# Chunked attention and a gated feed-forward network on one core: the down projection of the last 3584 tokens done with seven products instead of eight

## The chip, the cores and the metric

The kernel runs on one core of one Trainium2 chip. The metric is the device time of one execution in microseconds (us). TensorE (PE) multiplies matrices, VectorE (DVE), ScalarE (ACT) and GpSimd (POOL) work on elements, SyncE (SP) and ScalarE issue the transfers (DMA). The times of the kernel before are the median of three runs; everything that is said of single instructions comes from one profiled execution.

## The reference

The reference is, cut to what is computed:

```python
scores = scale * np.matmul(q_c, k_c.transpose(0, 1, 2, 4, 3))   # q, k, v: 8 x 8 heads x 576 x 64,
scores = scores - np.max(scores, axis=-1, keepdims=True)        # in chunks of 64 tokens
attn = np.exp(scores)
attn = attn / (np.sum(attn, axis=-1, keepdims=True) + 1e-09)
x = merge_heads(np.matmul(attn, v_c))                           # 4608 tokens x 512
h = x @ w_in                                                    # 512 x 2048
sp = np.where(h > 20.0, h, np.log1p(np.exp(np.minimum(h, 20.0))))
g = h * np.tanh(sp)                                             # Mish
return (g @ w_out).astype(np.float32)                           # 2048 x 512
```

The weights arrive as 64-bit words and are made into floats on the chip.

## The kernel before

**Precision.** Every large product is made of three matmuls on numbers that are split into a high part (a rounded copy, made by ScalarE) and a low part (what the copy left, a subtraction by VectorE): high by high, high by low, low by high. So each operand of a matmul costs one copy and one subtraction (`g_hi`, `g_lo`; `x_hi`, `x_lo`; `s_hi`, `s_lo`; `t_hi`, `t_lo`).

**Plain stage, the first 1024 tokens.** They go in two blocks of 512 tokens. A slot (`slot`, L811) takes one of the 16 strips of 128 hidden units: TensorE multiplies the tokens by the strip of w_in into `h` (`up`, L308, 12 matmuls of 512 columns), ScalarE applies Mish, the result is split, and one slot later TensorE adds its share of the output into `o_o` (`down`, L346, 12 matmuls). In the first block's slots the weights are also brought in and split. In the second block's slots, the sums of w_in that the next stage needs are made (`t_sum` and `t_diff` on GpSimd, `t_hi`, `t_lo`), and all split weights are written back to DRAM (`keep_weights`, `dwi`, `dwo`).

**Seven-product stage, the last 3584 tokens.** They go in four blocks of 896 tokens, each cut into two halves of 448. For a pair of 128-unit strips of w_in (a set; 8 sets a block, 32 in all) the product of 2 x 2 blocks is made from seven products instead of eight (`s_up`, L686; its matmuls stand at L699, 6 of 448 columns for each product). The operands of the seven products are sums of the blocks of x (`x_sum`, made once for each block of tokens) and of w_in. Their results are added up partly in PSUM, partly by VectorE (`s_copy` on ScalarE and `s_c`, L775, on VectorE); out come four pieces of h, called 11, 12, 21 and 22, each of 128 units by 448 tokens. Each gets Mish and is split (`s_hi`, L784 and L785; `s_lo`, L788). The down projection is plain here: for each of the 7 tiles of 128 tokens, 6 matmuls of 512 columns (`s_down`, L716; matmuls at L721) give the set's share of the output, which VectorE adds to a running sum (`s_out`, L748; in a block's first set ScalarE copies it instead, L746).

**What sets the order.** The order is written out by hand. The table `ORDER` has 14 steps for a set: seven products of the up projection with seven groups of the down projection of earlier sets in between, so that TensorE has a group of down work between any two products. `plan_set` (L919) hangs each element-wise operation on a step. `plan_x` (L937) hangs the conversion of the next block of x on the last set of a block: there GpSimd makes the sums and four of the seven low parts. `plan_pair` (L950) hangs the attention of ten later pairs of token tiles on steps of the running sets. Each engine works through its own instructions strictly in that order. The weights of the up projection come back from DRAM in groups of four products (`ring_load`), those of the down projection once for each set (`wo_load`), all by SyncE's queue.

## Time and profile before

| | |
|---|---|
| median of the three runs | 844.61 us (843.84 to 846.90) |
| the profiled execution's own time | 842.41 us |
| its span, first to last instruction | 840.6 us |
| TensorE busy | 829.7 us, 99% |
| VectorE busy | 507.0 us, 60% |
| ScalarE busy | 419.9 us, 50% |
| GpSimd busy | 111.0 us, 13% |
| transfers | 170.82 MB, 203 GB/s on average |
| granted TensorE clock | 1.00 all through |

In a row of the profile's groups stand the line, the engine, the operation, output and inputs by the program's names, the shapes, how often it occurs, its busy time and the mean of one in ns, and behind the last bar the idle time of the engine just ahead of it. "PEld" is the loading of TensorE's weights, which runs beside its matmuls. In the chain of waits and in a timeline a row gives start and duration in us. A window's row gives the busy time of each engine in that stretch.

### The profile page before, as it was taken

Reading aid. Unit: us, or ns where it says so; the run is one execution under the profiler, and the core shown is the slowest. Engines: PE = TensorE matmul, PEld = TensorE weight load, DVE = VectorE, ACT = ScalarE, POOL = GpSimd, SP = SyncE. Lnnn points to the kernel's source line nnn. Section 1 sums busy time; section 2 is a strip of 40 time slices with the busy share of each in tenths; the row PEclk is TensorE's granted clock in tenths of the full one; section 3 lists DMA queues with packets and bytes.
Section 4 is the critical chain, followed back from the end, with each engine's and each line's share of the span. In section 5 each row is a group of like instructions: output and inputs, shape, how many; then the busy total and the mean of one; then the engine's idle time right before and its main releaser. Section 6 shows DMA issues by size and latency. Waiting matters only on the chain.

```text
span 840.6 us, 14583 instructions
## 1 busy us (share of the span) xinstructions
PE 829.7 (99%) x5974; PEld 706.9 (84%) x5974; DVE 507.0 (60%) x784; ACT 419.9 (50%) x702; POOL 111.0 (13%) x83
## 2 busy tenths in 40 slices
PE   8999999999999999999999999999999999999997
PEld 7778878888888888888888888888888888888886
DVE  6898875666845656574555556544656563445444
ACT  6988855245573535554635545363535544433321
POOL 2100072652000000340000024100000440000000
PEclk9999999999999999999999999999999999999999
DMA  8767778988774644547545434764544456444413
GB/s 304 249 176 241 229 243 292 348 275 302 236 256 168 228 157 182 201 159 257 225 176 201 177 121 147 276 245 166 228 156 180 151 161 227 150 154 163 179 57 87
DMA packets 51298, 170.82 MB, mean 203 GB/s; under 512 B 5152, under 2 KB 11296, under 8 KB 39968
## 3 DMA queue, kind: packets, MB, share of 16 engines
q1 hardware_dynamic: 50384, 168.45, 57.5%
q10 hardware_dynamic: 848, 1.44, 0.4%
q8 instruction: 47, 0.77, 0.4%
q14 instruction: 19, 0.16, 0.0%
HBM read 137.36 MB, written 32.51 MB: 202 GB/s over the span
## 4 chain that ended last, share of the span: by engine, by line
PE 88%; DVE 4%; ACT 4%; DMA 2%; issue 2%; POOL 0%; ACTq 0%; POOLq 0%
PE d L721 36%; PE al L699 19%; PE g L699 9%; PE o_o L346 7%; PE h L308 6%; PE b L699 5%; PE av L182 2%; PE s L182 2%; PE pt L604 1%; DVE w L137 1%; DVE woc L126 1%; PE pt L251 1%; DMA wos<-in_w_out 1%; DMA wis<-in_w_in 1%; ACT woc L104 1%
## 5 line engine op out<-in xcount | busy, mean ns | idle before, releaser
L721 PE MATMUL d<-wo,g 128*128 128x512 f32 x1320 | 338.8, 392 | 0.0
L721 PEld LDWEIGHTS d<-wo,g 128*128 128x128 f32 x1320 | 247.9, 188 | 44.5
L748 DVE TENSOR_TENSOR sum<-d,sum 128x512 f32<-128x512 f32 x192 | 132.6, 691 | 185.7 <-PE d L721 184.9
L699 PE MATMUL al<-xo,ring 128*128 128x448 f32 x768 | 178.0, 367 | 0.0
L699 PEld LDWEIGHTS al<-xo,ring 128*128 128x128 f32 x768 | 142.4, 188 | 18.4 <-DVE c L775 0.7
L308 PE MATMUL h<-x,w 128*128 128x512 f32 (+1 forms) x396 | 93.9, 386 | 1.3 <-ACT x L282 0.8
L699 PE MATMUL g<-xo,ring 128*128 128x448 f32 x372 | 85.8, 366 | 0.0
L308 PEld LDWEIGHTS h<-x,w 128*128 128x128 f32 x396 | 71.8, 188 | 15.9 <-ACT x L282 0.9
L346 PE MATMUL o_o<-w,gh 128*128 128x512 f32 x256 | 79.0, 390 | 0.0
L699 PEld LDWEIGHTS g<-xo,ring 128*128 128x128 f32 x372 | 69.5, 188 | 8.4
L648 POOL TENSOR_TENSOR xs<-x 128x896 f32<-128x896 f32 x3 | 6.4, 2119 | 389.5 <-ACT x L545 389.5
L346 PEld LDWEIGHTS o_o<-w,gh 128*128 128x128 f32 x256 | 48.1, 188 | 9.7
L784 ACT ACTIVATE b<-b 128x448 f32<-128x448 f32 x31 | 16.4, 528 | 73.9 <-DVE b L775 73.9
L346 PE MATMUL o_o<-w,gl 128*128 128x512 f32 x128 | 50.8, 397 | 1.4 <-DVE gl L333 1.4
L784 ACT ACTIVATE g<-g 128x448 f32<-128x448 f32 x31 | 16.4, 528 | 69.8 <-DVE g L775 69.8
L699 PE MATMUL b<-xo,ring 128*128 128x448 f32 x186 | 43.4, 369 | 0.0
L784 ACT ACTIVATE c<-c 128x448 f32<-128x448 f32 x34 | 19.7, 578 | 37.1 <-DVE c L775 37.1
L699 PEld LDWEIGHTS b<-xo,ring 128*128 128x128 f32 x186 | 34.3, 188 | 3.6
L763 ACT COPY p<-al 128x448 f32<-128x448 f32 x32 | 17.1, 533 | 37.5 <-PE al L699 37.3
L494 POOL TENSOR_TENSOR c<-w 128x512 f32<-128x512 f32 x16 | 23.9, 1508 | 84.3 <-DVE w L137 84.3
L333 DVE TENSOR_TENSOR gl<-z,gh 128x512 fp32r<-128x512 f32 x32 | 27.7, 864 | 11.3 <-ACT gh L326 10.7
L775 DVE TENSOR_TENSOR b<-b,p 128x448 f32<-128x448 f32 x31 | 19.5, 629 | 22.7 <-PE b L699 22.2
(110 smaller groups left out, 985.3 us busy)
## 6 DMA issues: line engine op xcount, KB each, us to landing
ring<-dwi SPq DMA_DIRECT2D x56, 1024.0 KB, 4.9
wo<-dwo SPq DMA_DIRECT2D x32, 1024.0 KB, 4.8
wis<-in_w_in SPq DMA_DIRECT2D x16, 512.0 KB, 4.7
wos<-in_w_out SPq DMA_DIRECT2D x16, 512.0 KB, 3.7
q<-in_q SPq DMA_DIRECT2D x16, 512.0 KB, 5.9
k<-in_k SPq DMA_DIRECT2D x16, 512.0 KB, 6.7
v<-in_v SPq DMA_DIRECT2D x16, 512.0 KB, 5.8
dwo<-w SPq DMA_DIRECT2D x16, 512.0 KB, 6.8
```

Of the source, the lines that this page charges most:

```text
L104: nc.scalar.activation(out=c.bitcast(F32), in_=a[:, :, 1].bitcast(F32), func=AF.Copy, scale=2.0**-112)
L182: nc.tensor.matmul(o[h * CHUNK : (h + 1) * CHUNK, c, t - ts.start, g], lhsT=l[rows, t, 2 * g + h], rhs=r[rows, t, 2 * g + h], start=True, ...
L308: nc.tensor.matmul(h[:, cols], lhsT=wi(f, w_, kt), rhs=x[:, kt, cols], start=(n == 0), stop=(n == 3 * NK - 1),)
L333: nc.vector.tensor_tensor(out=d["gl"], in0=d["z"], in1=d["gh"].bitcast(F32), op=ALU.subtract)
L346: nc.tensor.matmul(acc[t], lhsT=g[:, sl], rhs=w_part(f, w_), start=(f == 0 and n == 0), stop=(f == NF - 1 and n == 2),)
L494: nc.gpsimd.tensor_tensor(out=d[e], in0=raw(w_part(f, 0)), in1=raw(w_part(f, 1)), op=ALU.add)
L699: nc.tensor.matmul(o[:, :HALF], lhsT=w_[:, wn, kt * P : (kt + 1) * P], rhs=x[:, xn, kt], start=(n == 0 and k < 3), stop=(n == 5), skip_gro ...
L721: nc.tensor.matmul(o, lhsT=g_tile(z, e)[:, gn, i * P : (i + 1) * P], rhs=wos[z % 2][:, e, wn], start=(n == 0), stop=(n == 5),)
L748: nc.vector.tensor_tensor(out=a, in0=o, in1=a, op=ALU.add)
L763: nc.scalar.copy(out=o, in_=(places["g"] if n == "p5" else places["a", z])[:, :HALF])
L775: nc.vector.tensor_tensor(out=ct[z, n], in0=o[:, :HALF], in1=ct.pop((z, other)), op=ALU.add)
L784: nc.scalar.activation(out=ct[z, n], in_=ct[z, n], func=AF.Mish)
```

## The change

**The down projection.** It now uses seven products of 2 x 2 blocks too. Its operands are sums of the four pieces of a set: T1 = 12 - 22, T3 = a copy of 11 - 12, T2 = that copy - T1, T4 = 21 - T2 (`s_t`), so a set now yields seven split pieces (11, 21, 22, T1 to T4) where there were four. Three of the low parts, T2 and T3 are made by GpSimd (`on_pool`), the rest by VectorE. The matching sums of w_out are made in the plain stage with those of w_in (`t_sum` now on VectorE and for both matrices, `t_diff` on GpSimd). The weights are now the stationary operand, so the output comes out turned: two sets together take 14 groups, each of 6 matmuls of 448 columns (`s_down(n)`), in the order `DOWN`; each is added to a running total by `s_out`, and in a block's last pair of sets VectorE also transposes it in squares of 32 before it is stored (`s_store`). The output columns of w_out are regrouped to suit this (`w_cols`).

**The order.** The up products of a set go in the order 0 1 3 2 5 4 6. The down groups of a pair of sets start 3 steps into the second set behind it, so the first two sets have no down group but those left over from the plain stage, and 15 groups stand alone at the end. The next block of x is converted over two sets, with all low parts and three of the four sums on VectorE.

**Plain stage.** In the second block Mish is applied in place in PSUM and `g_hi` is always ScalarE's; tiles have become views of fixed rooms.

On TensorE, in the middle of the seven-product stage, `al`, `b` and `g` are the up projection's banks and `d` the down projection's. Before:

```order
L699 MATMUL al_4483<-xo_2403,ring_2268 128x448 x6
L721 MATMUL d_2631<-wo_2481,g_2493 128x512 x3
L721 MATMUL d_2631<-wo_2481,g_2550 128x512 x3
L699 MATMUL b<-xo_2406,ring_2268 128x448 x6
L721 MATMUL d_2632<-wo_2646,g_2658 128x512 x3
L721 MATMUL d_2632<-wo_2646,g_2715 128x512 x3
```

and with the change, at the same place:

```order
L809 MATMUL al_5252<-xo,ring 128x448 x6
L927 MATMUL d_2543<-xo,wo 128x448
L927 MATMUL d_2543<-u,wo 128x448 x2
L927 MATMUL d_2543<-g,wo 128x448
L927 MATMUL d_2543<-yr,wo 128x448 x2
L809 MATMUL b<-xo,ring 128x448 x6
```

A down group still has six matmuls between two up products, and they have 448 columns where they had 512.

On VectorE, in the last set of a block, where the next block's x is converted (`xo` is the converted x, `x32` and here `x` the block it is read from, `sum` and `sums` the running totals, L788 and L887 the low parts). Before:

```order
L657 TENSOR_TENSOR xo0_2403<-x32_1_2446,xo0_2403 128x896
L775 TENSOR_TENSOR b_2629<-b_2629,p1_7_3613 128x448
L748 TENSOR_TENSOR sum0_2666<-d0_2631,sum0_2666 128x512
L788 TENSOR_TENSOR g2_2658<-b_2629,g2_2658 128x448
L657 TENSOR_TENSOR xo1_2406<-x32_1_2446,xo1_2406 128x896
L748 TENSOR_TENSOR sum0_2666<-d1_2632,sum0_2666 128x512
L748 TENSOR_TENSOR sum2_2700<-d0_2631,sum2_2700 128x512
L657 TENSOR_TENSOR xo3_2453<-x32_1_2446,xo3_2453 128x896
```

and with the change:

```order
L863 TENSOR_TENSOR b_2335<-b_2335,sums_81 128x448
L776 TENSOR_TENSOR xo_83<-x32_1398,xo_83 128x896
L955 TENSOR_TENSOR sums_81<-d1_2544,sums_81 128x14x32
L887 TENSOR_TENSOR u_84<-y_2329,u_84 128x448
L770 TENSOR_TENSOR x32_1398<-x32_1398 128x2x448
L770 TENSOR_TENSOR x32_1398<-xs_1_3487,x32_1398 128x2x448
L955 TENSOR_TENSOR sums_81<-d0_2543,sums_81 128x14x32
L887 TENSOR_TENSOR yr_2330<-b_2335,u_84 128x448
L776 TENSOR_TENSOR xo_83<-x32_1398,xo_83 128x896
L770 TENSOR_TENSOR x32_1398<-x32_1398 128x2x448
L955 TENSOR_TENSOR sums_81<-d1_2544,sums_81 128x14x32
```

The sums of x (L770), which stood on GpSimd, now stand between the additions of the down groups (L955).

On GpSimd there was nothing between two conversions of x. With the change, this is what stands for one set behind the sum of x (`y` and `z` are rooms for pieces, `g`, `xo`, `yr` and `u` rooms for split pieces; L909 is a T, L887 a low part):

```order
L770 TENSOR_TENSOR xs_1_3487<-x32_1398 128x896
L887 TENSOR_TENSOR u_84<-y_2329,u_84 128x448
L887 TENSOR_TENSOR g_80<-z_79,yr_2330 128x448
L909 TENSOR_TENSOR z_79<-y_2329,z_79 128x448
L909 TENSOR_TENSOR y_2329<-y_2329 128x448
L887 TENSOR_TENSOR xo_83<-z_79,u_84 128x448
```

So GpSimd now has five operations in every set, and has one left, the sum `xs`, in the conversion of a block.

The core of the diff (x_hi, the placing of the rooms, the weights' sums and the attention's moved steps are left out):

```diff
     def mish(i):
         d = it[i]
-        d["z"] = ew.tile([P, TOK], F32, name=f"z_{i}", tag="z", bufs=2)
+        d["z"] = z_turns.next([TOK]) if i < NF else d["h"]
         nc.scalar.activation(out=d["z"], in_=d["h"], func=AF.Mish)
...
-        if i < NF or i == N - 1:
-            nc.scalar.copy(out=d["gh"], in_=d["z"])
-        else:
-            nc.vector.tensor_copy(out=d["gh"], in_=d["z"])
+        d["gh"] = gh_turns.next([TOK], F32R)
...
+    UP = (0, 1, 3, 2, 5, 4, 6)
+    DOWN = (5, 3, 2, 1, 6, 7, 4)
+    NY = NS // 2
...
-    dwo = [dr.tile([P, 2, 2, DM], F32R, name=f"dwo_{s}") for s in range(NS)]
+    dwo = [dr.tile([P, len(DOWN), 2, 2, 2 * P], F32R, name=f"dwo_{y}") for y in range(NY)]
...
+    def t_sum(m, s):
+        d = tw[m, s] = {}
+        part = 2 * (m == "o")
...
         for e in range(2):
-            d[e] = wst.tile([P, DM], F32, name=f"c{e}_{s}", tag="c")
             f = 2 * s + e
-            nc.gpsimd.tensor_tensor(
-                out=d[e], in0=raw(w_part(f, 0)), in1=raw(w_part(f, 1)), op=ALU.add
+            nc.vector.tensor_tensor(
+                out=d[e], in0=raw(w_part(f, part)), in1=raw(w_part(f, part + 1)), op=ALU.add
             )
...
-        engine = nc.gpsimd if b else nc.vector
+        engine = nc.gpsimd if k == (2 if b else 4) else nc.vector
         engine.tensor_tensor(out=o, in0=l, in1=r, op=op)
...
-    def x_lo(b, k):
-        engine = nc.gpsimd if b and k in LOW_BY_POOL else nc.vector
-        engine.tensor_tensor(
-            out=xo[k][:, 1], in0=x_src(b, k), in1=raw(xo[k][:, 0]), op=ALU.subtract
...
+    def x_lo(b, k, cols=ALL):
+        nc.vector.tensor_tensor(
+            out=xo[k][:, 1, :, cols],
+            in0=x_src(b, k, cols),
+            in1=raw(xo[k][:, 0, :, cols]),
+            op=ALU.subtract,
+        )
...
+    def s_c(z, n):
+
+        where, other = {11: ("b", "p1"), 12: ("g", "u2"), 22: (("a", z), "p5")}[n]
+        o = places[where][:, :HALF]
+        if n != 22:
+            at_ps[z, n] = o
+        nc.vector.tensor_tensor(
+            out=take(z, 22) if n == 22 else o, in0=o, in1=held[z, other][1], op=ALU.add
+        )
+        give(z, other)
...
+    def s_t(z, n):
+
+        a, b = {
+            "T3": ((z, "r11"), (z, 12)),
+            "T1": ((z, 12), (z, 22)),
+            "T2": ((z, "r11"), (z, "T1")),
+            "T4": ((z, 21), (z, "T2")),
+        }[n]
+        l, r = source(*a), source(*b)
...
+
+    def on_pool(z, n):
+        return n in ("=T3", "=T2", 22, "T2", "T3")
+
+    UNIT_OF = {5: "T1", 3: 11, 2: 21, 1: 22, 6: "T2", 7: "T3", 4: "T4"}
+    PART_OF = {5: (1, 0), 3: (0, 0), 2: (0, 1), 1: (0, 1), 6: (0, 0), 7: (1, 0), 4: (1, 1)}
+
+    def s_down(n):
+
+        y, r = divmod(n, 2 * len(DOWN))
+        kk, h = divmod(r, 2)
+        k = DOWN[kk]
+        o = places["d", h]
+        m = 0
+        for i in range(2):
+            hi, lo = (u[1] for u in units[2 * y + i, UNIT_OF[k]])
+            for part, x in ((0, lo), (1, hi), (0, hi)):
                 nc.tensor.matmul(
-                    o,
-                    lhsT=g_tile(z, e)[:, gn, i * P : (i + 1) * P],
-                    rhs=wos[z % 2][:, e, wn],
-                    start=(n == 0),
-                    stop=(n == 5),
+                    o[:, :HALF],
+                    lhsT=wos[(len(DOWN) * y + kk) % 4][:, i, part, h * P : (h + 1) * P],
+                    rhs=x,
+                    start=(m == 0 and k in (5, 2, 1)),
+                    stop=(m == 5),
+                    skip_group_check=True,
                 )
-                n += 1
-
-    sums = {}
-
...
+    def s_out(n):
+        y, r = divmod(n, 2 * len(DOWN))
+        kk, h = divmod(r, 2)
+        k = DOWN[kk]
+        b, last = divmod(y, NY)
+        part, half = PART_OF[k]
+        o = totals[half][:, :, 2 * part + h]
+        i = places["d", h][:, :HALF].rearrange("p (b n) -> p b n", n=32)
+        if last == 0 and k in (5, 3, 2, 4):
+            nc.scalar.copy(out=o, in_=i)
             return
-        nc.vector.tensor_tensor(out=a, in0=o, in1=a, op=ALU.add)
-        if s == NS - 1:
...
+        nc.vector.tensor_tensor(out=o, in0=i, in1=o, op=ALU.add)
+        if last < NY - 1 or k not in (1, 6, 7, 4):
+            return
+        nc.vector.transpose(out=o, in_=o)
+        if b < NSB - 1:
+            if h == 1 and k in (7, 4):
+                s_store(b, half, slice(0, 4))
+        elif h == 1:
+            s_store(b, half, slice(2 * part, 2 * part + 2))
+
+    def s_store(b, half, js):
+        first = FIRST_TILE + b * BT
+        first = first * P + half * HALF
+        rows = out[first : first + HALF].rearrange("(b i) (a j n) -> a i b j n", i=32, a=4, j=4)
+        for a in range(4):
+            queue = nc.scalar if b == NSB - 1 and a % 2 else nc.sync
+            queue.dma_start(
+                out=rows[a, :, :, js].rearrange("i b j n -> i b (j n)"),
+                in_=totals[half][32 * a : 32 * a + 32, :, js].rearrange("p b j n -> p b (j n)"),
+            )
 
...
+        def at_(m, *ops):
+            when(*divmod(STEPS * z + m, STEPS), *ops)
+
+        at_(0, lambda: s_copy(z, "p1", ("a", z)))
+        at_(2, lambda: s_c(z, 11), lambda: s_mish(z, 11))
+        at_(3, lambda: s_hi(z, 11))
+        at_(4, lambda: s_copy(z, "u2", ("a", z)))
+        at_(5, lambda: s_raw(z), lambda: s_lo(z, 11))
+        at_(6, lambda: s_copy(z, "p5", "g"))
+        at_(8, lambda: s_c(z, 22), lambda: s_mish(z, 22))
+        at_(9, lambda: s_hi(z, 22))
+        at_(10, lambda: s_c(z, 12), lambda: s_mish(z, 12), lambda: s_lo(z, 22))
+        at_(11, lambda: s_t(z, "T1"), lambda: s_t(z, "T3"))
+        at_(12, lambda: s_mish(z, 21), lambda: s_hi(z, 21), lambda: s_hi(z, "T1"), lambda: s_hi(z, "T3"))
+        at_(13, lambda: s_t(z, "T2"), lambda: s_lo(z, 21), lambda: s_lo(z, "T1"), lambda: s_lo(z, "T3"))
+        at_(15, lambda: s_t(z, "T4"), lambda: s_hi(z, "T2"), lambda: s_lo(z, "T2"))
+        at_(17, lambda: s_hi(z, "T4"), lambda: s_lo(z, "T4"))
         if s == NS - 1 and b + 1 < NSB:
...
+        for k, m in (0, 1), (1, 3), (3, 6), (2, 8), (5, 10), (4, 12), (6, 14):
+            when(*divmod(STEPS * z + m, STEPS), lambda k=k: x_hi(b, k))
+        for k, m in (0, 2), (1, 5), (3, 8), (2, 13), (5, 15), (4, 17), (6, 19):
+            when(*divmod(STEPS * z + m, STEPS), lambda k=k: x_lo(b, k))
+        for k, m in (2, 0), (5, 3), (3, 4), (4, 6):
+            when(z, m, lambda k=k: x_sum(b, k))
...
     def s_set(z):
-        for m, (kind, i) in enumerate(ORDER):
-            back = {"u": 0, "d": 1, "e": 2}[kind]
-            if kind == "u":
-                if z < NSB * NS:
-                    s_up(z, i)
-            elif 0 <= z - back < NSB * NS:
-                s_down(z - back, i)
+        for m in range(STEPS):
+            i, odd = divmod(m, 2)
+            n = 7 * z + i - STEPS - LAG
+            there = odd and 0 <= n < NSB * NY * STEPS
+            if not odd and z < ZN:
+                s_up(z, i)
+            if there:
+                s_down(n)
             for op in pe.pop((z, m), ()):
```

More of the change, by code (lines that the diff above doesn't have):

```diff
@@ L518, in t_lo @@
+    def t_lo(m, s):
+        d = tw.pop((m, s))
         for i in range(2):
             o = d["s", i]
[L520 to L535 removed]
@@ L777, in g_view @@
[L777 to L790 removed]
+    wide = Free(
+        [("y", i * UNIT) for i in range(5)] + [("z", 0), ("z", UNIT), ("sums", 14 * KB)]
+    )
@@ new lines, with take, give, s_copy @@
+    held = {}
+    units = {}
+    def take(z, n):
+        held[z, n] = wide.take([HALF])
+        return held[z, n][1]
+    def give(z, n):
+        wide.give(held.pop((z, n))[0])
+    def s_copy(z, n, where):
+        nc.scalar.copy(out=take(z, n), in_=places[where][:, :HALF])
+    at_ps = {}
+    def s_c(z, n):
[5 more added lines that the diff above has]
+            out=take(z, 22) if n == 22 else o, in0=o, in1=held[z, other][1], op=ALU.add
+        )
+        give(z, other)
@@ L806 @@
             quick.setdefault(k0 + m, {})[name] = j
+    JOBS = {}
+    for n in range(2 * NS - 1):
+        JOBS[NF - 2 + n] = ("io"[n % 2], n // 2)
     N = NB * NF
@@ L866, in slot @@
             a_hi(a["x"])
-        if s < N:
+        if s < NF:
             g_hi(s)
@@ new lines @@
+        for at_step, i, ts in (
+            ((0, 1), N - 2, (0, 1)),
+            ((0, 5), N - 2, (2, 3)),
+            ((0, 9), N - 1, (0, 1)),
+            ((1, 3), N - 1, (2, 3)),
+        ):
+            pe[at_step] = [lambda i=i, ts=ts: down(i, ts)]
+            if i == N - 1:
+                when(*at_step, lambda ts=ts: store(NB - 1, ts))
+        when(0, 11, *(lambda n=n: wo_load(n) for n in range(4)))
+        slot(N - 1)
+        y_open()
+        banks_a.close()
+        ps_b = ctx.enter_context(tc.tile_pool(name="ps_b", bufs=1, space=bass.MemoryType.PSUM))
@@ L1027 @@
+        for n in "b", "g":
+            places[n] = ps_b.tile([P, DM], F32, name=n, tag=n)
+        for j, then in zip(range(AHEAD[-1] + 1, NPAIR), EXPS):
+            plan_pair(j, then)
+        for m, step in (5, t_sum), (6, t_diff), (22, t_hi), (25, t_lo):
+            when(*divmod(m, STEPS), lambda step=step: step(*LAST_JOB))
+        for z in 2, 17:
+            when(z, 2, x_late)
         for z in range(ZN):
             plan_set(z)
-        s_set(0)
-        plain.close()
-        ps_s = ctx.enter_context(tc.tile_pool(name="ps_s", bufs=1, space=bass.MemoryType.PSUM))
```

585 lines of the change are left out of this document (320 added, 265 removed).

## The prediction

> **What bounds the kernel now.** First the page's head: who is busy.
>
> ```profile
> span 840.6 us, 14583 instructions
> PE 829.7 (99%) x5974; PEld 706.9 (84%) x5974; DVE 507.0 (60%) x784; ACT 419.9 (50%) x702; POOL 111.0 (13%) x83
> ```
>
> TensorE is busy for 99% of the span, so the question for every edit is whether it shortens TensorE's own work and whether TensorE then has to wait. An average can hide stages, so next the windows: the plain stage with the weights, the plain stage with the sums of weights, the passage into the seven-product stage, and the three conversions of x.
>
> ```profile
> 25.00:106.00 81.00, 79.30 (x590) 64.61 (x589) 71.44 (x108) 70.28 (x117) 0.01 (x1) 1.00 0.70 220
> 106.00:213.00 107.00, 105.73 (x949) 86.44 (x948) 71.85 (x83) 47.94 (x69) 52.26 (x48) 1.00 0.83 284
> 213.00:245.00 32.00, 32.00 (x209) 27.89 (x208) 22.96 (x36) 22.56 (x38) 0.00 (x0) 1.00 0.85 283
> 334.00:372.00 38.00, 38.00 (x294) 32.67 (x293) 23.98 (x32) 17.37 (x29) 16.87 (x8) 1.00 0.50 186
> sum 143.00, PE 143.00 PEld 123.04 DVE 92.49 ACT 76.31 POOL 51.40; mean PE 35.75 PEld 30.76 DVE 23.12 ACT 19.08 POOL 12.85
> ```
>
> The columns behind the stretch are TensorE, weight loads, VectorE, ScalarE, GpSimd, granted clock, DMA share, GB/s. From 213 us on TensorE never pauses, at a granted clock of 1.00; the last row sums the passage (213 to 245) and the three conversions (334 to 372, 495 to 530, 648 to 686). Even where VectorE is 88% busy (71.44 of 81 us) TensorE loses 1.7 us. So the sum is TensorE's work, plus waits that the change brings in.
>
> Third, the chain of waits in the middle of a set, as it runs on TensorE alone.
>
> ```profile
> 402.08 1.38 PE d L721 x6
> 403.46 1.21 PE al L699 x6
> ...
> 419.02 1.21 PE al L699 x6
> 420.23 0.93 PE d L721 x4
> ```
>
> A product of the up projection (6 matmuls of 448 columns) takes 1.21 us, a group of the down projection (6 of 512) 1.38 us; seven of each take 420.23 - 402.08 = 18.15 us.
>
> **TensorE's part.** How many down groups there are:
>
> ```profile
> 0.00:840.60 840.60, 344.03 (x1344) 252.36 (x1344) 1.00 0.58 203
> ```
>
> That row counts line L721 alone: 1344 matmuls, 224 groups. The order shows as many groups with the change, each still 6 matmuls, now of 448 columns, the form of the up products. So a group falls from 1.38 to 1.21 us: 224 x 0.17 = **38.0 us less**. The attention, the plain stage and the up products keep their matmuls.
>
> **What it puts on the other engines.** The prices:
>
> ```profile
> L775 DVE TENSOR_TENSOR b<-b,p 128x448 f32<-128x448 f32 x31 | 19.5, 629 | 22.7 <-PE b L699 22.2
> L788 DVE TENSOR_TENSOR g<-al,g 128x448 fp32r<-128x448 f32 x29 | 17.8, 615 | 3.7 <-ACT g L785 3.7
> L785 ACT CAST g<-b 128x448 fp32r<-128x448 f32 x31 | 16.5, 534 | 1.0
> L648 POOL TENSOR_TENSOR x<-x 128x896 f32<-128x896 f32 x6 | 12.8, 2126 | 4.7 <-DVE xo L657 4.5
> ```
>
> On 448 columns VectorE takes 0.62 us an operation, ScalarE 0.53; GpSimd takes 2.13 on 896, so I estimate 1.06 on 448. A set now has on VectorE 7 additions of down groups, 3 of up products, T1 and T4, and 4 low parts: 16 x 0.62 = 9.9 us. ScalarE has 3 copies, 4 Mish, 7 high parts and the copy of 11: 15 x 0.53 = 8.0. GpSimd has T2, T3 and 3 low parts: 5.3. TensorE's set falls to 14 x 1.21 = 16.9 us, so in an ordinary set all fit.
>
> The catch is a resource that two engines share. At a conversion in the run before, VectorE's and GpSimd's timelines show:
>
> ```profile
> 357.61 2.10 POOL L657 TENSOR_TENSOR xo<-xs,xo 128x896 fp32r<-128x896 f32 x1
> ```
>
> ```profile
> 357.28 0.69 DVE L748 TENSOR_TENSOR sum<-d,sum 128x512 f32<-128x512 f32 x1 [1.32 <-PE d L721]
> 357.89 2.77 DVE L657 TENSOR_TENSOR xo<-x,xo 128x896 fp32r<-128x896 f32 x1
> 360.58 0.62 DVE L775 TENSOR_TENSOR g<-g,u 128x448 f32<-128x448 f32 x1
> ```
>
> VectorE's low part of x, issued at 357.89, ends at 360.66: 0.95 us after GpSimd's operation ended at 359.71. In the groups of the stretch from 245 to 800 us the same shows in two rows:
>
> ```profile
> L657 DVE TENSOR_TENSOR xo<-x,xo 128x896 fp32r<-128x896 f32 x9 | 14.8, 1647 | 0.7 <-ACT xo L653 0.7
> L788 DVE TENSOR_TENSOR g<-c,g 128x448 fp32r<-128x448 f32 x29 | 22.6, 779 | 0.7 <-ACT g L785 0.7
> L657 DVE TENSOR_TENSOR xo<-xs,xo 128x896 fp32r<-128x896 f32 x1 | 1.1, 1085 | 0.0
> ```
>
> Undisturbed the first takes 1.085 us (third row, at a time when GpSimd rests); 14.8 - 9 x 1.085 = 5.0 us were waits. The second, both of whose inputs lie in SBUF, has 22.6 - 29 x 0.615 = 4.8; its sister with an input in PSUM has none (615 on average, above). So GpSimd's 51.4 us of work at the conversions cost VectorE 9.8 us, 19%, and only operations with both inputs in SBUF pay.
>
> The Trainium skill (SBUF — State Buffer, "Who interferes with whom") says more: a VectorE instruction with two SBUF inputs and a GpSimd instruction that reads SBUF exclude each other, and the second to issue is blocked until the first is done. The row of 2.77 us agrees; by the rule taken to its end, with GpSimd never giving way, the sum would be that of the second rival below.
>
> **Conversions of x, three times.** They now spread over 20 steps of 1.21 us, 24.2 us. VectorE's own work in them is 9.9 x 20/14 = 14.2 us, and 7 low parts and 3 sums x 1.085 = 10.9: 25.1 us. GpSimd has 5.3 x 20/14 = 7.6 and the sum xs, 2.1: 9.7 us. In these steps 10 + 3 x 20/14 = 14 operations of VectorE have two SBUF inputs (T1 and the low parts of T1 and T4 in every set), against some 6 before, so I raise the 19% to a third: 3.2 us. That makes 28.3 us of 24.2: VectorE falls 4.1 us behind. Behind each delayed operation is queued the addition of a down group, for which TensorE waits: it uses two banks in turn, so an addition may end 3 steps after its group, 3.6 us, and needs 0.62: 3.0 us of cover. **1.1 us a conversion, 3.3 in all.** If nothing waits, the 0.9 us are covered: 0. If all of GpSimd's time is waited for, 25.1 + 9.7 - 24.2 - 3.0 = 7.6 each: 23.
>
> **The first two sets.** No down group runs there but four left over: TensorE needs 14 x 1.21 + 4 x 1.38 = 22.5 us, for which it had the work of one set before. ScalarE has 2 x 8.0, and seven more copies (high parts of x and of weight sums, stores) of 448 to 896 columns, some 5 us by their width: 21 of 22.5. A copy that freed a bank within three steps now has one product, 1.21 us, to hide behind; the first down group waits for T1 of the second set through additions, Mish, T1, high and low part, six operations of 0.5 to 0.6 one behind the other. Bounds: 0 (the window 213 to 245 was filled as well by VectorE, 72%, and TensorE did not pause) and about one operation lost at each of ten such places, 6 us. I take **2**.
>
> **The plain stage's second half.**
>
> ```profile
> L520 DVE TENSOR_TENSOR ts<-t,ts 128x512 fp32r<-128x512 f32 x16 | 13.6, 885 | 2.6 <-ACT ts L514 2.6
> L328 DVE CAST gh<-z 128x512 fp32r<-128x512 f32 x15 | 11.0, 733 | 9.3 <-PE o_o L346 9.3
> ```
>
> VectorE gets 30 sums of weights and 14 more low parts, 44 x 0.885 = 39 us at the price of the first row, waits included, and loses the 11.0 of the second: 72 + 28 = 100 of 107 us at worst. GpSimd gives up its sums. What TensorE waits for, the low part of the hidden units, now reads PSUM, and may be a whole slot late. **0.5**, bounds 0 and 4.
>
> **The end.**
>
> ```profile
> 834.98 0.69 DVE L748 TENSOR_TENSOR sum<-b,sum 128x512 f32<-128x512 f32 x1 [0.67 <-PE b L721]
> 836.33 0.69 DVE L748 TENSOR_TENSOR sum<-g,sum 128x512 f32<-128x512 f32 x1 [0.67 <-PE g L721]
> out<-sum SPq DMA_DIRECT2D x49, 128.0 KB, 2.5
> ```
>
> ```profile
> L566 DVE TENSOR_REDUCE m<-s 128x8 f32<-128x512 f32 x20 | 13.6, 682 | 6.5 <-PE s L182 6.5
> 167.92 0.42 DVE L328 CAST gh<-z 128x512 fp32r<-128x512 f32 x1
> ```
>
> Behind the last addition (837.0) 3.6 us go to the last store. Now a transpose stands behind it, which no row shows; 0.4 us (the copy of the last row) and 1.4 (twice the reduction's 0.68) bound it. The last eight groups run at 1.21 us each against addition and transpose on VectorE, 1.0 to 2.0, and the store is in runs of 256 bytes. I take **1.5**, bounds 0.5 and 6.
>
> The Trainium skill (DMA: Bandwidth & Descriptors, "Specifications") puts the least transfer for full rate at 512 bytes; no row of before shows what less costs. By it the end is rather 3 and the sum 1.5 more.
>
> **Covered.** The loads of down weights grow from 32 of 1024 KB to 112 of 512 KB; each is asked for three products ahead, 12 x 1.21 = 14.5 us:
>
> ```profile
> wo<-dwo SPq DMA_DIRECT2D x32, 1024.0 KB, 4.8
> ```
>
> Landing takes 4.8 us, and less per load; SyncE's stores, which wait for VectorE's transposes, stand ahead of some and may be 9 us late. Uncovered, each would cost its lateness. Pairs of attention add VectorE work in the sets between; GpSimd's third of 5.3 us is 1.8 a set: **0.5** in all, bounds 0 and 5.
>
> **Sum** against the profiled execution's 842.4: - 38.0 + 3.3 + 2 + 0.5 + 1.5 + 0.5 = 812.2. The median of the runs lies 2.2 above that execution, so **814.4**, which I write as 814.
>
> **Rivals.**
> 1. *No wait appears.* For it: TensorE did not pause in any window, 72% and 88% of VectorE notwithstanding. Against: no stretch before asked VectorE for more than its time, and a conversion now asks for 25.1 of 24.2 us ahead of any wait. 842.4 - 38.0 + 1.5 + 2.2 = 808. Chance 0.25.
> 2. *VectorE and GpSimd exclude each other at every meeting,* and the conversions bind: 23 in place of 3.3, and 4 at the first sets: 836. For it: 357.89. Against: 19%, not 100%, of GpSimd's time was waited for. Chance 0.14. (This is the skill's rule of above.)
> 3. *Slower: VectorE becomes the bound of every set.* Its 9.9 us, and by set 10 x 6.3/32 = 2.0 for pairs (eight operations of 0.68 and some small ones), 1.0 for x and 0.6 for transposes, make 13.5; TensorE's set was 18.15 + 0.95 for pairs = 19.1. The change loses from 5.6 us of waits a set on, a little more than all of GpSimd's 5.3. GpSimd itself is slowed where they meet:
>
> ```profile
> L494 POOL TENSOR_TENSOR c<-w 128x512 f32<-128x512 f32 x16 | 23.9, 1508 | 84.3 <-DVE w L137 84.3
> ```
>
> The undisturbed 512 would take 1.2 us at the price above, so it stretches by a quarter: 6.6 us a set, all waited for, gives 20.1, 1.0 x 32 over before: 842.4 + 32 + 2.2 = 877. Against it: the same 19%. Chance 0.06.
>
> That the change does not do what it says is shut out by the order, which has the 448 columns.
>
> **Numbers.** The forecast has 0.55. The range 806 to 832 holds it and the first rival, 0.80, and leaves out most of the other two. Its low end is the first rival less 2, the distance between runs; its high end is 814 with 10 more for the conversions (halfway to their bound), 4 for the first sets and 4 for the end. 0.5% of 844.61 is 4.2 us, about what a measurement of this kernel can tell from no change. Faster by more than that: the forecast, the first rival, nearly all of the second, 0.90; within: a second rival at its end with late first sets, 0.03; slower 0.07.
>
> **What would show it.** Right: down groups at 1.21 us in the chain of waits; TensorE's idle in the middle of a block none, and up to 2 us near each conversion, released by VectorE's additions; stretched T1 and low parts of x on VectorE beside GpSimd. Wrong: down groups over 1.25 us would fell the 38; idle in every set would show the third rival; idle released by loads, the cover of 14.5 us.

## The result and the profile after

The changed kernel takes **820.1 us** (median of 4 runs, 819.3 to 820.8) against 844.4 before (four runs here, three in the table above): a ratio of 0.9706, 95% interval 0.9685 to 0.9727. That is 24.3 us faster; 30 were forecast, and 820 lies inside the range of 806 to 832. The profiled execution took 819.8 us, its span is 818.0. Its page begins:

```profile
span 818.0 us, 15365 instructions
PE 799.5 (98%) x5974; PEld 706.9 (86%) x5974; DVE 593.2 (73%) x929; ACT 489.2 (60%) x867; POOL 274.9 (34%) x239
```

TensorE's work fell by 30 us, and its share only from 99 to 98%: 18.5 us of the span are without it now, 10.9 before. The chain of waits in the middle of a set:

```profile
434.59 1.22 PE al L809 x6
435.81 1.21 PE d L927 x6
437.02 1.22 PE b L809 x6
```

A down group (L927) takes what a product of the up projection (L809) takes, as forecast, and nothing waits there. TensorE's own timeline shows where it does wait in the passage; the bracket holds the idle time and what ended it:

```profile
238.32 1.49 PE L809 MATMUL al<-xo,ring 128*128 128x448 f32 x6 [0.82 <-ACT y L853]
246.14 0.47 PE L927 MATMUL d<-u,wo 128*128 128x448 f32 x1 [0.87 <-DVE u L887]
```

Both stand where the prediction put its 2 us: a product whose bank ScalarE had not yet copied, and the first down group, which waits for the low part of T1. The stretch at which the prediction did not look closely is the plain stage's second half, where the attention of four pairs of token tiles is also done (the quick pairs, ahead of the ten later ones). Its windows, before and then after (TensorE, weight loads, VectorE, ScalarE, GpSimd, clock, DMA share, GB/s):

```profile
140.00:170.00 30.00, 30.00 (x264) 24.60 (x256) 22.26 (x22) 10.91 (x15) 18.30 (x18) 1.00 0.99 340
170.00:217.00 47.00, 47.00 (x392) 38.75 (x392) 32.30 (x38) 22.33 (x32) 17.34 (x16) 1.00 0.78 265
```

```profile
140.00:170.00 30.00, 27.79 (x265) 22.52 (x257) 23.79 (x31) 15.41 (x23) 17.52 (x18) 1.00 1.03 351
170.00:217.00 47.00, 46.40 (x387) 37.69 (x386) 35.72 (x48) 29.14 (x44) 22.07 (x25) 1.00 1.01 363
```

No engine is full, but the transfers are: the sums of down weights go out too, and the DMA share is 1.03 and 1.01. In the first row it was 0.99 before as well, and nothing waited. TensorE now loses 2.2 us in the first row and 0.6 in the second, where it had lost none. One of the two longest of these waits, 1.1 us, is for k of the third quick pair. The load's issue by SyncE and its time to landing (the last number), before and then after:

```profile
156.03 0.38 SPq L164 DMA_DIRECT2D k<-in_k  x1
k<-in_k SPq DMA_DIRECT2D x1, 512.0 KB, 5.5
```

```profile
160.56 0.54 SPq L237 DMA_DIRECT2D k<-in_k  x1
k<-in_k SPq DMA_DIRECT2D x1, 512.0 KB, 6.3
```

So k lands 5.3 us later, and 4.5 of them come from its issue: from 148.3 to 158.4 us SyncE issues stores of weights and their sums without a pause, 11 between the load ahead and these two where there were 9. From issue to landing k takes 0.8 us longer. It is much the same for q, issued at 158.4 instead of 153.2 us and landed 7.1 us later instead of 6.5.

To sum up, the intervals from the start of one matmul to the start of the next were added up in both traces, each counted above the ordinary one of its kind (0.203 us for 448 columns, 0.230 for 512), and set beside the forecast:

| | forecast | measured |
|---|---|---|
| columns: 1344 matmuls of 0.230 to 0.203 | -38.0 | -36.8 |
| start of the execution (differs from one to the next) | 0 | +0.8 |
| plain stage | +0.5 | +2.9 |
| passage, first two sets | +2 | +2.0 |
| three conversions of x | +3.3 | +0.5 |
| later pairs of attention (the prediction's "covered") | +0.5 | +4.2 |
| what is left, single intervals longer by under 0.15 us | 0 | +2.0 |
| the end | +1.5 | +1.8 |
| sum, span to span | -30.2 | -22.6 |

The medians differ by more, 24.3 us, because the profiled execution of before lay 2.0 us under its median and that of after only 0.3.

### The profile page after: what moved, and what is told of

Read it like the earlier page. It is cut to its first block, busy times and chain, and to the rows that moved or that the text cites. A ratio compares the mean times of both kernels' runs of the same rounds, so it can differ in the third digit from the quotient of the medians.

```text
span 818.0 us, 15365 instructions
## 1 busy us (share of the span) xinstructions
PE 799.5 (98%) x5974; PEld 706.9 (86%) x5974; DVE 593.2 (73%) x929; ACT 489.2 (60%) x867; POOL 274.9 (34%) x239
## 4 chain that ended last, share of the span: by engine, by line
PE 75%; DVE 11%; DMA 5%; ACT 5%; issue 2%; SPq 1%; POOL 0%; ACTq 0%; POOLq 0%
PE d L927 30%; PE al L809 17%; PE g L809 9%; PE o_o L416 5%; PE h L381 4%; PE b L809 4%; PE av L255 2%; PE s L255 2%; DMA k<-in_k 1%; DVE sums L955 1%; DMA dwi<-sums 1%; DVE sums L958 1%; DMA ring<-dwi 1%; PE pt L719 1%; DVE r L308 1%
## 5 line engine op out<-in xcount | busy, mean ns | idle before, releaser
L927 PE MATMUL d<-u,wo 128*128 128x448 f32 x800 | 207.3, 367 | 1.2 <-DVE u L887 0.9
L955 DVE TENSOR_TENSOR sums<-d,sums 128x448 f32<-128x448 f32 x192 | 119.3, 621 | 96.1 <-PE d L927 95.2
L809 PE MATMUL al<-xo,ring 128*128 128x448 f32 x768 | 177.3, 367 | 0.8 <-ACT y L853 0.8
L927 PEld LDWEIGHTS d<-u,wo 128*128 128x128 f32 x800 | 149.5, 188 | 14.5 <-DVE sums L955 1.4
L809 PEld LDWEIGHTS al<-xo,ring 128*128 128x128 f32 x768 | 143.4, 188 | 13.9 <-ACT y L853 2.0
L809 PE MATMUL g<-xo,ring 128*128 128x448 f32 x384 | 88.7, 366 | 0.0
L809 PEld LDWEIGHTS g<-xo,ring 128*128 128x128 f32 x384 | 71.7, 188 | 5.8
L927 PE MATMUL d<-g,wo 128*128 128x448 f32 x194 | 57.2, 365 | 0.0
L927 PE MATMUL d<-yr,wo 128*128 128x448 f32 x184 | 56.2, 369 | 0.0
L927 PE MATMUL d<-xo,wo 128*128 128x448 f32 x166 | 51.3, 368 | 0.0
L887 POOL TENSOR_TENSOR u<-y,u 128x448 fp32r<-128x448 f32 x20 | 24.3, 1216 | 78.4 <-ACT u L881 78.4
L909 POOL TENSOR_TENSOR z<-y,z 128x448 f32<-128x448 f32 x27 | 32.7, 1210 | 44.3 <-DVE y L909 36.7
L809 PE MATMUL b<-xo,ring 128*128 128x448 f32 x192 | 44.7, 368 | 0.0
L887 POOL TENSOR_TENSOR g<-y,yr 128x448 fp32r<-128x448 f32 x10 | 11.6, 1158 | 94.0 <-ACT yr L881 94.0
L381 PE MATMUL h<-x,xo 128*128 128x512 f32 x168 | 41.2, 394 | 0.0
L416 PE MATMUL o_o<-xo,g 128*128 128x512 f32 x168 | 41.0, 393 | 0.0
L927 PEld LDWEIGHTS d<-g,wo 128*128 128x128 f32 x194 | 36.4, 188 | 2.9
L809 PEld LDWEIGHTS b<-xo,ring 128*128 128x128 f32 x192 | 35.7, 188 | 3.1
L927 PEld LDWEIGHTS d<-yr,wo 128*128 128x128 f32 x184 | 34.5, 188 | 3.7 <-DVE sums L955 0.6
```

Of the source, the lines that this page charges most:

```text
L381: nc.tensor.matmul(h[:, cols], lhsT=wi(f, w_, kt), rhs=x[:, kt, cols], start=(n == 0), stop=(n == 3 * NK - 1),)
L416: nc.tensor.matmul(acc[t], lhsT=g[:, sl], rhs=w_part(f, w_), start=(f == 0 and n == 0), stop=(f == NF - 1 and n == 2),)
L809: nc.tensor.matmul(o[:, :HALF], lhsT=w_[:, wn, kt * P : (kt + 1) * P], rhs=x[:, xn, kt], start=(n == 0 and k < 3), stop=(n == 5), skip_gro ...
L887: engine.tensor_tensor(out=u[1][1], in0=source(z, n), in1=raw(u[0][1]), op=ALU.subtract)
L909: engine.tensor_tensor(out=o, in0=l, in1=r, op=ALU.subtract)
L927: nc.tensor.matmul(o[:, :HALF], lhsT=wos[(len(DOWN) * y + kk) % 4][:, i, part, h * P : (h + 1) * P], rhs=x, start=(m == 0 and k in (5, 2, 1)),
```

## The experiments

The theory after the result: the columns give all that they promise, and the rest is waits of TensorE for VectorE's order and for transfers. The rivals: TensorE itself gains less than the columns say, or GpSimd's and VectorE's exclusion takes the gain back.

**1. The columns alone.** The kernel before, shorter down matmuls and nothing else:

```diff
+        cols = slice(0, DM if z < 2 or z == NSB * NS - 1 else HALF)
-        o = d_bank(z, i)
+        o = d_bank(z, i)[:, cols]
-                    rhs=wos[z % 2][:, e, wn],
+                    rhs=wos[z % 2][:, e, wn, cols],
```

> The kernel before, with 448 instead of 512 columns in the matmuls of the down projection of 29 of its 32 sets; it leaves out the last 64 columns of those sums. Nothing else changes. My theory: columns alone give the gain of the change, 0.164 us a group (1.382 to 1.218 as the two traces have it), 203 groups: 33.3 us less, 811 against 844.4, and no wait appears, since VectorE has as much work as before. Rival: part of the change's missing gain is TensorE's own, a matmul of 448 columns that follows another down matmul being held up by its weight load; then a matmul stays above 0.203 us and the time ends at 815 or above.

Measured: 811.1 us (810.0 to 811.8), ratio 0.9608 (0.9587 to 0.9629), 32.8 us less where 33.3 were expected. The columns' price holds; the rest of the change costs some 12 us elsewhere (36.8 for all 32 sets, less the 24.3 between the medians).

**2. The quick pairs' softmax where it was.**

```diff
             up(s + 1, last="w")
+        if "norm" in e:
+            a_norm(e["norm"])
...
-            a_inverse(e["norm"])
-            a_norm(e["norm"])
...
+        if "max" in e:
+            a_inverse(e["max"])
```

> The changed kernel, with the sums and products of the four quick pairs' softmax back at the places they had before (the sums at the end of one slot, the product at the start of the next). My theory: the four waits of TensorE for the product, ahead of the transposes (0.69, 1.47, 0.69, 0.69 us where 0.25 is the ordinary interval), come from this place alone: 0.4 + 1.2 + 0.4 + 0.4 = 2.5 us less, 817.6, and the first up product of the seven-product stage starts at about 216 instead of 218.47. Rival: VectorE is late there because of the sums of the weights and the low parts of the hidden units that it took over; then the waits stay or move to the first down products of the slots, and the time stays at 820.

Measured: 823.9 us, 0.9764 (0.9739 to 0.979): 4 slower than the changed kernel. My theory fell. The transposes now wait longer, and VectorE's timeline shows why:

```profile
153.44 1.06 PE L324 MATMUL pt<-ident,p 128*128 128x128 f32 x8 [1.30 <-DVE p L315]
```

```profile
147.01 1.22 DVE L308 TENSOR_REDUCE r<-p 128x16 f32<-128x1024 f32 x1 [3.27 <-ACT p L303]
...
148.65 0.63 DVE L578 TENSOR_TENSOR c<-wo 128x512 f32<-128x512 f32 x1
149.20 0.68 DVE L578 TENSOR_TENSOR c<-xo 128x512 f32<-128x512 f32 x1
149.79 1.83 DVE L628 TENSOR_TENSOR sums<-z,sums 128x512 fp32r<-128x512 f32 x2
151.54 1.75 DVE L315 TENSOR_TENSOR p<-p,r 128x1024 f32<-128x1024 f32 x1
```

The sums of the softmax (L308 to L310) stand first in the queue and wait 3.27 us for ScalarE's exponential; the weight work behind them, which could have run in that time, runs after it, ahead of the product (L315). An engine takes its instructions in order, so the place of a waiting one costs what stands behind it.

**3. The sums between.** From that: weight sums first, then the softmax's sums, then the low parts of the weights.

```diff
-            a_inverse(e["norm"])
...
             t_sum(*JOBS[s])
+        if "max" in e:
+            a_inverse(e["max"])
         if behind:
             t_lo(*behind)
```

> The changed kernel, with the quick pairs' sums and reciprocals placed on VectorE between the sums of the weights and the low parts of the weights, one slot earlier than now; the product by the reciprocals and the transposes stay. My theory after the last runs: VectorE stands idle there for 2 us in each of these slots, because its next instruction, a low part, waits for ScalarE's copy, which waits for a store; 1.6 us of sums put in that hole bring the product 1.1 us forward: the waits of TensorE at the transposes (0.44 + 1.22 + 0.44 + 0.44 above the ordinary interval) fall to at most 0.2 each, 818 against 820. Rival: VectorE as a whole is full in these slots, and what is put ahead delays the low parts and with them the next product by as much: 820 or more.

Measured: 819.2 us, 0.9706 (0.9688 to 0.9725). The four waits are gone from the trace, 2.5 us, as expected, but this row of TensorE has grown from a wait of 1.1 us:

```profile
166.17 1.16 PE L255 MATMUL s<-k,q 64*64 64x64 f32 x64 [2.37 <-DMA k<-in_k]
```

The scores of the third quick pair start between 166.2 and 168.3 us in eleven of the twelve kernels with seven down products, whatever stands ahead of them, and in all of these but experiment 2's TensorE waits for the pair's loads there. A gain ahead of that point is mostly lost to it.

**4. k from another queue.** As 3, with the loads of q and k moved behind Mish and this:

```diff
+            load_qk(e["load"], queues=(nc.sync, nc.scalar))
```

> The kernel with the sums between (the run before of the quick pairs), and besides the quick pairs' loads of q and k issued after Mish instead of ahead of the weights, k from ScalarE's queue instead of SyncE's. My theory: k comes 2.8 us late at 163 us because it is issued at 160.6, behind stores and q on one queue, although its buffer is free at 157; from a queue of its own it is issued 3 us earlier and the wait of 2.4 us above the ordinary goes: 816.8 against 819.2. Rival: the DMA engines are full there (94% of the stretch), so k lands no earlier from another queue, and the stores behind it come later: 819 or more.

Measured: 823.1 us, 0.9755 (0.974 to 0.9771), 4 slower than 3. The rival's figure came true, but not its reason: k was issued at 157.9 us, where 3 had issued it at 159.4, and landed 1.8 us earlier, at 164.2. Now q is late: SyncE still issued it at 159.5, and it took 7.0 us to land where it had taken 5.8 in 3.

```profile
166.78 1.98 PE L255 MATMUL s<-k,q 64*64 64x64 f32 x64 [2.94 <-DMA q<-in_q]
168.70 1.67 PE L381 MATMUL h<-x,xo 128*128 128x512 f32 x4
```

**5. Transposes of the later pairs one step later.**

```diff
-            at_(then + 11, lambda t=t: p_copy(j, t))
-        on_pe(then + 10, lambda: p_transpose(j))
+            at_(then + 12, lambda t=t: p_copy(j, t))
+        on_pe(then + 11, lambda: p_transpose(j))
```

> The changed kernel, with the transposes of the ten later pairs of attention one step later on TensorE (1.2 us), and the copies behind them one step later on ScalarE; the values stay. My theory: the transposes wait up to 1.1 us for VectorE's products, which stand behind low parts that GpSimd held up; one step more covers it: 2.5 us less, 817.6, with no transpose above 0.2 us. Rival: VectorE falls behind for longer than a step; then the wait goes to the values two steps on (copies of 0.6 us each now have 2 steps instead of 3) and the time stays at 820.

Measured: 818.7 us (817.1 to 821.0), 0.9699 (0.9676 to 0.9722). The summary of the transposes' line, changed kernel first, says what ended TensorE's waits (us, times):

```profile
L719 PE MATMUL pt<-ident,c x80: 270/272/333, 272.6 to 606.5; 128*128 128x128 f32 x80
...
its engine sat idle before it (us, times) until:
  DVE c L709: 4.6, 7
```

```profile
L719 PE MATMUL pt<-ident,c x80: 270/272/273, 274.5 to 606.2; 128*128 128x128 f32 x80
...
its engine sat idle before it (us, times) until:
who waited for it (us, times):
```

All waits are gone (in intervals 2.9 us), so the place is right; the time fell by about half of it, within the spread of the runs. The reason that I gave was wrong, though. At the longest wait (388 us, changed kernel) GpSimd rests, and VectorE works without a pause on something new, the transposes of a block's last sums (L958):

```profile
386.53 0.62 DVE L887 TENSOR_TENSOR xo<-b,u 128x448 fp32r<-128x448 f32 x1
387.07 0.61 DVE L955 TENSOR_TENSOR sums<-d,sums 128x448 f32<-128x448 f32 x1
387.71 0.65 DVE L958 STREAM_TRANSPOSE sums<-sums 128x448 f32<-128x448 f32 x1
388.28 0.65 DVE L709 TENSOR_TENSOR c<-c,r 128x512 f32<-128x512 f32 x1
```

**6. More of GpSimd in the conversions.**

```diff
-        nc.vector.tensor_tensor(
+        engine = nc.gpsimd if b and k in (2, 4, 5, 6) else nc.vector
+        engine.tensor_tensor(
```

> The changed kernel, with four of the seven low parts of each of the three conversions on GpSimd, as they were before. My theory: GpSimd's work is waited for only in part (19% before, up to a third here); VectorE sheds 4 x 1.1 = 4.3 us and gets at most 2.8 us of waits in each conversion: same time, 820, plus or minus 1. Rival, full exclusion: 4 x 2.1 = 8.5 us more of GpSimd in each conversion are waited for by VectorE, 4.2 more than it sheds, about 12 us in the three: 826 to 832.

Measured: 819.8 us, 0.9726 (0.9694 to 0.9758): the same. The first conversion, changed kernel and then this one; GpSimd's column is the fifth:

```profile
341.00:366.00 25.00, 25.00 (x124) 22.86 (x123) 23.88 (x31) 15.45 (x27) 10.00 (x7) 1.00 0.68 231
```

```profile
345.00:370.00 25.00, 25.00 (x125) 22.97 (x124) 23.40 (x32) 16.69 (x30) 13.34 (x10) 1.00 0.68 226
```

TensorE pauses in neither. In the 28 us from the sum `xs` on, GpSimd has 19 us of work in each conversion here, against 10 in the changed kernel. But VectorE's operations that then take over 0.1 us more than alone lose 3.4, 2.3 and 2.3 us in sum, against 4.1, 3.0 and 3.0. Exclusion at every meeting as the bound of the conversions is out. (The profiled execution of this kernel was the slowest of its four, 825.1 us; most of that is a wait of 2.6 us for k of the third quick pair and the halved clock behind it, not the conversions.)

**7. GpSimd left out of the sets.**

```diff
-        return n in ("=T3", "=T2", 22, "T2", "T3")
+        return False
```

> The changed kernel, with T2, T3 and the three low parts that GpSimd computes in each set on VectorE. My theory: GpSimd's help is worth more than its waits cost: VectorE gets 5 x 0.62 = 3.1 us a set more and stands at 16.6 of 17.9 us in a set with attention, TensorE waits in some sets: 822 to 830. Rival (exclusion nearly complete): VectorE loses to GpSimd about as much as GpSimd does for it, so nothing changes: 818 to 821.

Measured: 827.3 us, 0.9802 (0.9787 to 0.9818). GpSimd's help is worth 7 us, waits included, as my theory had it. The waits come at block ends (two transposes wait 1.6 us each, 0.8 in the changed kernel), in the passage and in the first conversion, with VectorE at 79% of the span.

**8. The passage.**

```diff
-                when(*at_step, lambda ts=ts: store(NB - 1, ts))
+                when(at_step[0], at_step[1] + 4 * at_step[0], lambda ts=ts: store(NB - 1, ts))
-        for m, step in (5, t_sum), (6, t_diff), (22, t_hi), (25, t_lo):
+        for m, step in (5, t_sum), (6, t_diff), (22, t_hi), (28, t_lo):
-    EXPS = (41, 62, ...
+    EXPS = (42, 62, ...
```

> The changed kernel, with the last two stores of the plain stage four steps later in the second set, the low parts of the last job on the weights three steps later, and the first late pair of attention one step later. My theory: the two waits of the passage, 0.99 us at the seventh product of the second set and 1.03 at the first down group, are ScalarE's and VectorE's queues: a store's copy of 0.59 us ahead of the copy that frees the bank, and two low parts of 1.1 us, stretched by GpSimd, ahead of the low part of T1. Both shrink: 0.5 and 1.0 us less, 818.5. Rival: the chain through additions, Mish, T1, high and low part is itself too long for one product of cover, and the waits stay: 820.

Measured: 826.8 us, 0.9797 (0.9781 to 0.9812): 7 slower. The two waits did fall as expected, from 0.99 and 1.03 to 0.38 and 0.27. But the low parts' store releases the buffers that the first later pair loads into (in the changed kernel its k waits 3.8 us in SyncE's queue for that store). Its q now goes out 4.6 us later, right ahead of k, and k, issued 0.6 us later, takes 7.1 us to land instead of 3.8:

```profile
257.07 1.21 PE L255 MATMUL s<-k,q 64*64 64x64 f32 x37 [3.03 <-DMA k<-in_k]
```

**9. The end in runs of 512 bytes.**

```diff
-        if b < NSB - 1:
-            if h == 1 and k in (7, 4):
-                s_store(b, half, slice(0, 4))
-        elif h == 1:
-            s_store(b, half, slice(2 * part, 2 * part + 2))
+        if h == 1 and k in (7, 4):
+            s_store(b, half, slice(0, 4))
```

> The changed kernel, with the last block stored as the other blocks are, half by half in runs of 512 bytes and not quarter by quarter in runs of 256. My theory: the end costs 1.84 us more than before, 0.65 of it the transpose behind the last addition and 1.2 the slower landing of runs of 256 bytes; with 512 the last store has twice the bytes (0.92 MB) at up to twice the rate: the end within 0.5 us of now, 820. Rival: the short runs cost nothing and the bytes alone count: twice the bytes behind the last transpose, 2 to 3 us more, 822 to 823.

Measured: 823.4 us, 0.9758 (0.974 to 0.9776); the rival was right, if a little low. Last transpose and stores (KB each, median us to landing), the changed kernel and then this one:

```profile
812.54 0.65 DVE L958 STREAM_TRANSPOSE sums<-sums 128x448 f32<-128x448 f32 x1
out<-sums SPq DMA_DIRECT2D x8, 112.0 KB, 3.1
```

```profile
813.58 0.65 DVE L958 STREAM_TRANSPOSE sums<-sums 128x448 f32<-128x448 f32 x1
out<-sums SPq DMA_DIRECT2D x4, 224.0 KB, 5.7
```

From the last transpose's end to the span's end it is 4.8 us there and 8.9 here (span 823.1). Twice the bytes behind the last work cost far more than longer runs save.

**10 to 12. Together.** Three kernels join 3 and 5 with later pairs' loads three steps earlier (`start - 10`), the store's move of 8 and other steps for the last job's high and low parts.

```diff
-        at_(start - 7, lambda: p_load(j))
+        at_(start - 10, lambda: p_load(j))
-        for m, step in (5, t_sum), (6, t_diff), (22, t_hi), (25, t_lo):
+        for m, step in (5, t_sum), (6, t_diff), (10, t_hi), (13, t_lo):
```

> The changed kernel with all that helped and what the misses taught: the sums between, k of the quick pairs from ScalarE's queue, the transposes of the later pairs one step later, the loads of the later pairs three steps earlier, the last two stores of the plain stage four steps later, and the last job's high and low parts in the first set (steps 10 and 13) instead of the second (22 and 25). My theory: 2.5 (quick transposes) + 2.0 (k of the quick pairs) + 2.3 (transposes of later pairs) + 1.2 (passage) + 1.5 (k of later pairs) = 9.5 less, though part of each comes back in other waits as in the single runs (there half to two thirds was kept): 814. Rival: VectorE's and the DMA's queues are full, each gain returns as the next wait: 818 or more.

Measured (this one with the queue of 4): 817.9 us (817.2 to 822.3), 0.9717 (0.9694 to 0.974). Between the two expectations: every wait of the later pairs is gone, but q is late at 165 us, and the first wait of the passage has grown to 1.4.

> As the kernel with all together, but k of the quick pairs back on SyncE's queue, and the last job's low parts at step 19 (between the low part of the eleventh sum of the second set and its next addition, when GpSimd rests) instead of 13. My theory: against the changed kernel 0.9 kept at the quick pairs (the load of k stays late), 2.3 + 1.5 at the later pairs, 0.5 + 0.8 in the passage: 6 less, 814; waits left above half a microsecond behind 100 us: k at 163, the first passage wait at 0.3 to 0.6 above the ordinary interval, and 0.5 at the first conversion. Rival: the low parts in the second set delay another step of its chain and VectorE gives the gain back there: the passage as late as in the changed kernel, 815 to 817.

Measured (SyncE's queue, steps 10 and 19): **817.3 us** (816.8 to 820.4), 0.9689 (0.9676 to 0.9702), the lowest median of all, 2.8 under the changed kernel's; the intervals of the two overlap, so it is no shown gain. The rival's figure fits better, for another reason: in the profiled execution the passage waits are down to 0.5 and 0.3, but k of two pairs is late by 3.1 and 2.3. (That execution, at 820.4 us, was the slowest of the five.)

> As the last kernel, but every direct store of the weights starts three slots earlier (slots 8 to 23 instead of 11 to 26), and the last job's low parts stand at step 17. My theory: k of the third quick pair lands at 166 to 167 us in every run, whatever waits stand ahead, because the DMA engines are full from 140 to 217 us (shares of 1.03 and 1.01); the earlier stores use the share of 0.77 before that, k lands by 165, and TensorE waits there less than 1 us instead of 3.2 (with 2 us more of halved clock behind a wait that long). So the first up product of the seven-product stage starts at about 216 and the time is 814 to 815.5. Rival: k's landing hangs on its place in SyncE's queue and its buffer, and the stores push other loads later: 817 to 818, with the wait for k as long as now.

Measured (with `KEEP = 8`, step 17): 820.2 us, 0.9728 (0.9715 to 0.9741). My theory's numbers did not come, and the run missed its aim: the share falls only behind the load in question (140 to 170 us as full as before). The rival's reason fits, its figure does not: k was issued at 161.3 us, and TensorE waited 2.7 us for it.

```profile
140.00:170.00 30.00, 27.33 (x299) 22.37 (x298) 22.67 (x30) 16.48 (x25) 19.55 (x20) 0.99 1.01 353
170.00:217.00 47.00, 47.00 (x386) 38.51 (x386) 35.62 (x47) 28.22 (x42) 24.26 (x24) 0.97 0.81 289
```

So that full DMA engines set k's landing is not shown, and the traces speak for its place in SyncE's queue as the larger part. Where k stays on that queue, the changed kernels issue it at 158.8 to 162.1 us (156.0 before) and it lands 6.3 to 7.5 us later (5.5 before). A run that puts both q and k ahead of the stores was not made, and whether full engines also slow the issuing was not tried, so this stays open.

## Why the prediction was right, and where its steps were off

- **TensorE's part** was right: 36.8 us instead of 38.0, because 1.38 and 1.21 had been rounded (0.164 a group, not 0.17). Experiment 1 shows it by itself.
- **Conversions of x** were sized wrong, 3.3 against 0.5. The step that failed is "VectorE's own work in them is 14.2 us", at 0.62 an operation, 25.1 with those of x. An operation's duration is not its pace: in a full stretch the next begins before the last has ended, every 0.53 us, or 1.0 where the duration is 1.08. Rows of experiment 6:

```profile
348.72 0.61 DVE L910 TENSOR_TENSOR y<-al,y 128x448 f32<-128x448 f32 x1
349.25 0.62 DVE L864 TENSOR_TENSOR b<-b,sums 128x448 f32<-128x448 f32 x1
349.78 1.08 DVE L777 TENSOR_TENSOR xo<-x,xo 128x896 fp32r<-128x896 f32 x1
350.78 0.61 DVE L956 TENSOR_TENSOR sums<-d,sums 128x448 f32<-128x448 f32 x1
```

  At that pace the operations that the prediction counted take about 22 us (22.9 x 0.53 + 10 x 1.0), and with waits for GpSimd VectorE is busy for 23.9 of 25. The waits themselves were about as forecast, 4.1, 3.0 and 3.0 us for 3.2. At one meeting VectorE stands still for nearly all of GpSimd's operation (changed kernel):

```profile
340.88 2.17 POOL L770 TENSOR_TENSOR xs<-x 128x896 f32<-128x896 f32 x1
```

```profile
341.01 2.52 DVE L887 TENSOR_TENSOR u<-z,xo 128x448 fp32r<-128x448 f32 x1
```

  By the rule of the Trainium skill (SBUF — State Buffer, "Who interferes with whom") the two exclude each other. This meeting agrees; experiment 6 shows that its sum, the second rival, does not follow.

  The rest of the mechanism held, and more closely than 0.5 us suggests. VectorE's additions start up to 2.8 to 3.0 us behind their groups in the three conversions, so the cover of 3.0 us was used up. In each of them an addition ends just 0.06 us before TensorE uses its bank again:

```profile
352.44 0.62 DVE L955 TENSOR_TENSOR sums<-d,sums 128x448 f32<-128x448 f32 x1
```

```profile
353.12 0.46 PE L927 MATMUL d<-xo,wo 128*128 128x448 f32 x1
```

  The 0.5 us are six such matmuls, late by 0.06 to 0.11 each. One longer wait for an addition, 0.5 us at 328 us, stands a set ahead of the first conversion's first operation (340.88), behind the softmax of a pair, and is counted with the pairs.
- **The first two sets** were right in size, place and releaser; experiment 8 shows that two queues made them.
- **The plain stage's second half** was sized wrong, 0.5 against 2.9. It looked at VectorE's total, 100 of 107 us, and at the low part of the hidden units. What was late is the product ahead of the quick pairs' transposes (experiments 2 and 3: a matter of order), and behind it k.
- **Covered** failed in two steps, 0.5 against 4.2 and a part of the plain stage's 2.9. "Landing takes 4.8 us, and less per load" held for the loads of down weights (3.9 us), and that stores stand ahead of loads in SyncE's queue was seen for these loads alone; it was q and k of the pairs that were issued late, behind the stores of weights and their sums. And "GpSimd's third of 5.3 us is 1.8 a set: **0.5** in all" spread the pairs' cost over sets; 2.0 us of it came at the ends of two blocks, where VectorE's transposes of sums meet a pair's softmax (experiment 5).
- **The end** was right, 1.8 for 1.5, the transpose 0.65. The Trainium skill's least size for full rate (DMA: Bandwidth & Descriptors, "Specifications") points the right way, but here, by the queues' shares in the last 12 us, a packet of 256 bytes took 20 ns of a DMA engine and one of 512 took 34, 16% less per byte:

```profile
q10 hardware_dynamic: 3712, 0.92, 39.8%
q1 hardware_dynamic: 3712, 0.92, 37.7%
```

```profile
q10 hardware_dynamic: 1856, 0.92, 33.1%
q1 hardware_dynamic: 1856, 0.92, 32.0%
```

  (Packets, MB and the share of 16 engines in 12.2 us, the changed kernel and then experiment 9: 0.775 x 16 x 12.2 us / 7424 and 0.651 x 16 x 12.2 / 3712.) Waiting for longer runs lost (experiment 9).
- **Luck** had a part in the number. The conversions were put 2.8 us too high, which hid as much of what the other terms missed: with them at 0.5 the same sum gives 811.6, 8.5 us under the measured time instead of 5.7.
- **The rivals**: no wait appears (808) fell by the profile, exclusion (836) by experiment 6 and by the 3 to 4 us that VectorE lost beside some 10 us of GpSimd's work in a conversion, VectorE as the bound of every set (877) by the chain; experiment 7 shows how near it was in single places.
- The 2.0 us of single longer intervals have no experiment and stay open.

## What to carry to other kernels

When matmuls get shorter, price them by their interval from start to start, and the other engines' work by its pace in a full stretch, not by durations. Then look for the places where two one-off jobs meet (a block's end and a softmax, a weight store and a load), since the averages hide them. A wait that is taken away is a gain only up to the next thing that is late for a reason of its own, here loads that stand behind stores in a queue.
